# The last w_down rows as two column halves, three pieces loaded in parts by partitions, and 4 MB of w_o as one load

## Chip, cores and metric

One core of one Trainium2 chip. The time is the device time of one execution in microseconds (us), the median of several; the times of the kernel before lie within 0.1% of each other in one set of runs.

## The reference, cut to what matters

A decode step of one token: adaLN modulation, attention of 32 query heads over a cache of 4 x 65536 positions, then a gated feed-forward. The end of it is what the change touches:

```python
def _B_ref(x, w_gate, w_up, w_down):          # x: 1 x 1024, F = 3584
    return _gelu(x @ w_gate) * (x @ w_up) @ w_down
...
h = _layernorm(x, axis=-1) * (1 + cb) + sb
x = x + gb * _B_ref(h, B_w_gate, B_w_up, B_w_down)
```

Every weight and every cache row is used once, so the kernel is a stream of 185.6 MB from HBM into SBUF with the arithmetic beside it.

## The kernel before

All loads are planned in one list and issued in that order from SP. Each goes into a slot of a ring, is a single transfer over all 128 partitions, and adds 16 to a semaphore (the trace has 16 landing records for each of the last pieces):

```python
def issue_ready():
    while issued[0] < len(loads):
        j = loads[issued[0]]
        if any(q.freed is None for q in j.prev):
            return
        SP.wait(*(q.freed for q in j.prev))
        sp.dma_start(j.view, j.src).then_inc(j.tok[0], 16)
        issued[0] += 1
```

w_down comes last. The list, with the cuts of the last two blocks of 512 rows:

```python
j_o += [plan_o(16, 0), plan_o(24, 1)]                    # w_o: two of 2 MB
... # w_gate: two of 3.67 MB; w_up: two of 3.67 MB
wd_v = B_w_down.rearrange("(b p e) n -> p b e n", p=P, e=UE)   # b: 7 blocks, p: 128 partitions, e: 4 rows
... # two loads of two blocks (2 MB each), then
while b < NBF:
    for e, ne in ((0, UE),) if b < NROW else ((0, 2), (2, 2)) if b == NROW else ((0, 2), (2, 1), (3, 1)):
        ...  # 1 MB | 512 KB, 512 KB | 512 KB, 256 KB, 256 KB
```

The first five blocks are used as the moving operand (row matmuls, 512 columns); the last two as weights, so that the output falls into columns of PSUM that need no transpose:

```python
for kk in range(nk):
    for j in range(nblk):                                # nblk = 8
        ins = pe.matmul(
            bank[:, j:j + 1], view[:, kk, j:D:nblk], rhs[:, k0 + kk:k0 + kk + 1],
            start=first, stop=True, skip_group_check=True)
```

`view[:, kk, j:D:nblk]` is 128 weight columns, 8 elements (16 bytes) apart.

## Time and profile before

| | kernel before |
|---|---|
| time | 437.44 us (437.43 to 437.52, 3 runs) |
| span of the profiled run, granted clock | 436.2 us, 0.830 |
| HBM read | 185.60 MB at 426 GB/s over the span |
| landing of the 1 MB piece | 428.38 us |
| landing of the three 512 KB pieces | 429.62, 430.89, 432.13 us |
| landing of the two 256 KB pieces | 432.76, 433.40 us |
| end of the last matmul | 434.3 us |

A landing is the time at which the last of a load's 16 shares has come, read from its semaphore in the trace. TensorE in the last 8 us, as the timeline of the kernel before has it (start and length in us, engine, line, operation, tiles, shapes, count, and in brackets the idle time before it with what ended it):

```profile
428.42 1.06 PE L409 MATMUL kt_ps<-slots,p_row 128*32 128x512 bf16 x8 [1.38 <-DMA slots<-in_B_w_down_dram]
429.67 1.13 PE L386 MATMUL b<-p_row,slots 128*128 128x1 bf16 x16 [0.19 <-DMA slots<-in_B_w_down_dram]
430.92 0.29 PE L868 MATMUL b<-kt_sb,sel 128*32 128x8 f32 x8
431.14 3.14 PE L386 MATMUL b<-p_row,slots 128*128 128x1 bf16 x48
```

After 428.42 the brackets almost disappear: 48 column matmuls run without one. The windows of the kernel before (length, busy us of each engine with its count, granted clock, mean share of the DMA engines that are busy, GB/s) show the loads at their full rate almost to the end:

```profile
427.00:428.00 1.00, 0.04 (x4) 0.00 (x0) 0.00 (x0) 0.00 (x0) 0.00 (x0) 0.84 0.99 410
429.00:430.00 1.00, 0.81 (x13) 0.34 (x6) 0.45 (x1) 0.00 (x0) 0.00 (x0) 0.50 1.00 410
430.00:431.00 1.00, 0.88 (x20) 0.80 (x20) 0.86 (x2) 0.00 (x0) 0.00 (x0) 0.50 1.02 406
```

### The profile page before, as it was taken

To read this page: it belongs to the slowest core of one execution; us is meant where nothing else is said; L and a number is where in the kernel's file an instruction comes from. 1 tells how busy PE (TensorE), PEld (TensorE's weight loads), DVE (VectorE), ACT (ScalarE), POOL (GpSimd) and SP (SyncE) were. 2 spreads that over 40 slices of the span, in tenths; PEclk is the share of its full clock that TensorE was granted. 3 is DMA by queue.
4 is the path that set the end of the run, shared out by engine and by line. 5 is a ranking of instruction groups with operands and counts; after the bars stand their busy time and mean duration, and the time that the engine had idled before them with its cause. 6 is when DMAs were issued, how large, how long until landed. Compare 5 with 4: busy or idle time off the path is not lost.

```text
span 436.2 us, 8423 instructions
## 1 busy us (share of the span) xinstructions
PE 302.8 (69%) x3858; PEld 200.5 (46%) x3858; DVE 206.7 (47%) x303; ACT 111.2 (26%) x164; POOL 16.8 (4%) x23
## 2 busy tenths in 40 slices
PE   0435559959696878949787794969689596565366
PEld 0112236736464656636465563646456373232024
DVE  6601015637373755736474763738377465321001
ACT  1000001533332423333341353333235334000000
POOL 9500000000000000000000000000000000000000
PEclk9995569999796988988896897969689889578856
DMA  8999999999999999999999999999999999999996
GB/s 355 433 421 434 433 431 431 431 432 433 433 433 439 430 433 433 436 433 433 439 433 433 433 430 436 433 436 436 433 433 433 433 418 436 437 433 429 420 425 265
DMA packets 8192, 185.77 MB, mean 426 GB/s; under 512 B 1010, under 2 KB 1010, under 8 KB 1652
## 3 DMA queue, kind: packets, MB, share of 16 engines
q1 hardware_dynamic: 8176, 185.60, 99.0%
q8 instruction: 8, 0.13, 0.1%
q14 instruction: 4, 0.03, 0.0%
q10 hardware_dynamic: 4, 0.00, 0.0%
HBM read 185.60 MB, written 0.00 MB: 426 GB/s over the span
## 4 chain that ended last, share of the span: by engine, by line
DMA 56%; PE 31%; DVE 11%; issue 1%; ACT 1%; POOL 0%; POOLq 0%
DMA slots<-in_A_k_cache_dram 45%; PE kt_ps L575 16%; DMA slots<-in_B_w_down_dram 7%; PE b L645 4%; DMA slots<-in_A_v_cache_dram 4%; PE sc_ps L597 4%; PE kt_ps L409 3%; DVE selt L359 3%; DVE kt_sb L683 2%; DVE s_pad L717 1%; DVE o_red L706 1%; PE sc_ps L626 1%; PE b L613 1%; PE b L386 1%; DVE o_acc L694 1%
## 5 line engine op out<-in xcount | busy, mean ns | idle before, releaser
L575 PE MATMUL kt_ps<-ident,slots 128*128 128x128 bf16 x2048 | 156.7, 238 | 48.8 <-DMA slots<-in_A_k_cache_dram 48.0
L683 DVE COPY kt_sb<-kt_ps 128x2048 bf16<-128x2048 bf16 x96 | 117.6, 1225 | 111.5 <-PE kt_ps L575 109.9
L575 PEld LDWEIGHTS kt_ps<-ident,slots 128*128 128x128 bf16 x2048 | 136.1, 108 | 74.3 <-issue 41.9
L683 ACT ACTIVATE kt_sb<-kt_ps 128x2048 bf16<-128x2048 bf16 x32 | 60.1, 1877 | 27.7 <-PE kt_ps L575 27.7
L732 ACT ACTIVATE p_sb<-sc_ps 128x512 bf16<-128x512 bf16 x32 | 19.1, 597 | 182.4 <-PE sc_ps L626 182.4
L597 PE MATMUL sc_ps<-kt_sb,q_buf 128*32 128x512 bf16 x528 | 50.8, 420 | 0.0
L645 PE MATMUL b<-slots,p_sb 128*32 128x512 bf16 x560 | 40.1, 411 | 5.3 <-DMA slots<-in_A_v_cache_dram 4.6
L409 PE MATMUL kt_ps<-slots,h_pad 128*32 128x512 bf16 x176 | 19.1, 571 | 22.0 <-DMA slots<-in_B_w_up_dram 9.7
L694 DVE SCALAR_TENSOR_TENSOR o_acc<-o_acc,s_pad,b 128x512 f32<-128x512 f32 x28 | 20.9, 747 | 12.2 <-PE b L645 11.9
L613 PE MATMUL b<-m_sp,selt 128*128 128x16 f32 x66 | 13.0, 272 | 18.2 <-DVE m_sp L722 16.5
L645 PEld LDWEIGHTS b<-slots,p_sb 128*32 128x32 bf16 x560 | 15.5, 104 | 20.1 <-issue 5.1
L717 DVE TENSOR_REDUCE s_pad<-sc_ps 128x1 f32<-128x512 f32 x32 | 21.8, 682 | 0.0
L738 ACT ACTIVATE p_row<-sc_ps,s_pad 128x512 bf16<-128x512 f32 x32 | 21.7, 677 | 0.0
L409 PEld LDWEIGHTS kt_ps<-slots,h_pad 128*32 128x32 bf16 x176 | 6.3, 130 | 32.7 <-issue 11.9
L613 PEld LDWEIGHTS b<-m_sp,selt 128*128 128x128 f32 x66 | 9.8, 188 | 23.7 <-DVE m_sp L722 21.4
L597 PEld LDWEIGHTS sc_ps<-kt_sb,q_buf 128*32 128x32 bf16 x528 | 10.9, 95 | 12.3 <-issue 4.5
L409 PE MATMUL kt_ps<-slots,s_pad 128*32 128x512 bf16 x96 | 10.9, 516 | 7.5 <-DMA slots<-in_w_mod_dram 7.5
L452 POOL TENSOR_TENSOR rs<-va,halfneg 128x1 f32<-128x1 f32 x2 | 1.1, 555 | 375.7 <-DVE va L449 375.7
L793 DVE COPY kt_sb<-kt_ps 128x512 f32<-128x512 f32 x3 | 2.1, 692 | 27.7 <-PE kt_ps L409 27.7
L626 PEld LDWEIGHTS sc_ps<-ident,p_row 128*128 128x128 bf16 x136 | 7.8, 98 | 15.1 <-issue 14.4
L626 PE MATMUL sc_ps<-ident,p_row 128*128 128x128 bf16 x136 | 13.7, 224 | 0.2 <-ACT p_row L738 0.2
L727 DVE TENSOR_REDUCE s_pad<-b 128x1 f32<-128x16 f32 x32 | 5.6, 175 | 14.6 <-PE b L613 14.6
(98 smaller groups left out, 148.1 us busy)
## 6 DMA issues: line engine op xcount, KB each, us to landing
slots<-in_A_k_cache_dram SPq DMA_DIRECT2D x16, 4096.0 KB, 23.5
slots<-in_A_v_cache_dram SPq DMA_DIRECT2D x16, 4096.0 KB, 23.6
slots<-in_w_mod_dram SPq DMA_DIRECT2D x4, 3072.0 KB, 20.4
slots<-in_A_wq_dram SPq DMA_DIRECT2D x2, 4096.0 KB, 35.8
slots<-in_A_wo_dram SPq DMA_DIRECT2D x4, 2048.0 KB, 25.3
slots<-in_B_w_gate_dram SPq DMA_DIRECT2D x2, 3584.0 KB, 30.2
slots<-in_B_w_up_dram SPq DMA_DIRECT2D x2, 3584.0 KB, 29.5
slots<-in_B_w_down_dram SPq DMA_DIRECT2D x2, 2048.0 KB, 35.1
```

Of the source, the lines that this page charges most:

```text
L359: dve.tensor_scalar(selt[:, :].rearrange("p (r h) -> p r h", h=REP), selw[:, HQ - REP:HQ].unsqueeze(1).to_broadcast([P, NR, REP]), -scale, ...
L409: ins = pe.matmul(out, pad[:, k, :], view[:, kk, c0:c0 + ROW], start=k <= last_k[0], stop=k >= last_k[1], skip_group_check=True,)
L575: ins = pe.transpose(kt_ps[:, half * 2048 + t * P:half * 2048 + (t + 1) * P], j_k[i - i % KU].view[:, i % KU * CH + b * TB + t, :], ident[ ...
L597: ins = pe.matmul(sc(j)[QD * g:QD * (g + 1), :], q_buf[:, j % SITES, QD * b:QD * (b + 1)], kt_sb[:, j % 2, n:n + w, :].rearrange("p n d -> ...
L613: ins = pe.matmul(b6[:, 0:NR], selt[:, :], m_sp[:, j % 2, :], start=True, stop=True)
L626: ins = pe.transpose(sc_bf[:, o:o + P], p_row[:, j % 2, c * P:(c + 1) * P], ident[:, :])
L645: ins = pe.matmul(b7[QD * c:QD * (c + 1), :].rearrange("p (b d) -> p b d", b=NB), p_sb[:, s, c * P + QD * g:c * P + QD * (g + 1)], v[:, NQ ...
L683: ev[i % SITES][b].done(act.activation(dst, src, ACT.Copy) if E_ is AC else dve.tensor_copy(dst, src))
L694: v = oc[j % SITES].done(dve.scalar_tensor_tensor(o_acc[:, :], o_acc[:, :], al[:, j:j + 1], b7[:, :], ALU.mult, ALU.add))
L717: v = DVE.done(dve.tensor_reduce(m_new, sc(j), AX.X, ALU.max))
L732: pc[jt % SITES].done(act.activation(p_sb[:, jt % SITES, :], sc_bf[:, o:o + ROW], ACT.Copy))
L738: v_x[j] = ex[s].done(act.activation(p_row[:, j % 2, :], sc(j), ACT.Exp, bias=mneg[:, j:j + 1], scale=scale, accum_out=zr[:, j:j + 1],))
```

## The change

Its intent: the 16 DMA engines run dry at different times, up to 1.8 us apart (the shares of the last load land from 431.60 to 433.40), and a cut of 112 rows plus a few is meant to give the late ones less; the last 256 KB come as two column halves, so that less work is left after the last landing; and w_o's last two loads of 2 MB become one of 4 MB. The core of the diff:

```diff
-            sp.dma_start(j.view, j.src).then_inc(j.tok[0], 16)
+            p = 0
+            for n in j.cut:
+                sp.dma_start(j.view[p:p + n], j.src[p:p + n]).then_inc(j.tok[0], 16)
+                p += n
...
-        j_o += [plan_o(16, 0), plan_o(24, 1)]
+        j_o.append(plan_o(16, 0, 16))
...
                     jb = plan_load(
-                        wd_v[:, b, e:e + ne, :], flat(ne, D), jb.slot, beside=jb, off=(UE + e) * D, sem=9 - e)
+                        wd_v[:, b, e:e + ne, :], flat(ne, D), jb.slot, beside=jb, off=(UE + e) * D, sem=9 - e,
+                        cut=(112, 12, 4) if e == 0 else (112, 14, 2))
+                elif b + 1 == NBF and e == 0:
+                    jb = plan_load(wd_v[:, b, e:e + ne, :], flat(ne, D), next(tail_d), cut=(112, 10, 6))
+                elif b + 1 == NBF and e + 1 == UE:
+                    halves = [plan_load(
+                        wd_v[:, b, e:e + 1, h * ROW:(h + 1) * ROW], flat(1, ROW), next(tail_d)) for h in range(2)]
+                    break
...
-        v = col_matvec(acc_dn, late[1:], o_pad[:, :, 0], KD, False)
+        col_matvec(acc_dn, late[1:], o_pad[:, :, 0], KD, False)
+        for h, jb in enumerate(halves):
+            PE.wait(jb.tok)
+            for j in range(KD):
+                ins = pe.matmul(
+                    acc_dn[h * P // 2:(h + 1) * P // 2, j:j + 1], jb.view[:, 0, j:ROW:KD], o_pad[:, FD - 1:FD, 0],
+                    start=False, stop=True, skip_group_check=True)
```

More of the change, by code (lines that the diff above doesn't have):

```diff
@@ L198, in bass_adaLN_cond__gqa_block_cached__geglu_ffn__decode_kernel, with plan_load @@
     loads = []
-    def plan_load(src, view_fn, slot, site=None, nslot=1, beside=None, off=0, sem=None):
+    def plan_load(src, view_fn, slot, site=None, nslot=1, beside=None, off=0, sem=None, cut=(P,)):
         if site is not None:
@@ L206, in plan_load @@
             sem = slot if sem is None else sem
-            nfill[sem] += 1
+            nfill[sem] += len(cut)
             tok = (fill[sem], 16 * nfill[sem])
@@ L210, in plan_load @@
         job.src = src
+        job.cut = cut
         job.freed = None
@@ L264, in emit_all, with plan_o @@
         tail = iter([2, 4, 6, 8])
-        tail_d = iter([0, 1, 2, 3, 4, 5])
-        def plan_o(k, slot):
-            return (plan_load(wo_v[:, k:k + 8, :], flat(8, D), slot), k, 8)
+        tail_d = iter([0, 1, 2, 3, 4, 5, 6])
+        def plan_o(k, slot, n=8):
+            return (plan_load(wo_v[:, k:k + n, :], flat(n, D), slot, nslot=n // 8), k, n)
         def vslot(j):
@@ L870, in emit_all @@
                 start=False, stop=True, skip_group_check=True)
-        v = col_matvec(acc_dn, late[1:], o_pad[:, :, 0], KD, False)
+        col_matvec(acc_dn, late[1:], o_pad[:, :, 0], KD, False)
[5 more added lines that the diff above has]
+                    start=False, stop=True, skip_group_check=True)
+            v = PE.done(ins)
+            release(jb, v)
         DVE.wait(v)
```

## The prediction

> **What bounds the kernel now.** I read the page first, for the whole span.
>
> ```profile
> PEclk9995569999796988988896897969689889578856
> DMA  8999999999999999999999999999999999999996
> HBM read 185.60 MB, written 0.00 MB: 426 GB/s over the span
> DMA slots<-in_A_k_cache_dram 45%; PE kt_ps L575 16%; DMA slots<-in_B_w_down_dram 7%; PE b L645 4%; DMA slots<-in_A_v_cache_dram 4%; PE sc_ps L597 4%; PE kt_ps L409 3%; DVE selt L359 3%; DVE kt_sb L683 2%; DVE s_pad L717 1%; DVE o_red L706 1%; PE sc_ps L626 1%; PE b L613 1%; PE b L386 1%; DVE o_acc L694 1%
> ```
>
> The DMA engines are full in 38 of 40 slices: the kernel streams 185.6 MB, and neither kernel reads less. Only the two ends can move. So I read the chain of waits of the last 10 us (start, length, what):
>
> ```profile
> 397.44 30.93 DMA slots<-in_B_w_down_dram
> 428.38 0.04 issue
> 428.42 1.10 PE kt_ps L409 x8
> 429.52 0.03 issue
> 429.55 1.33 DVE kt_sb L860 x2
> 430.87 0.04 issue
> 430.92 0.29 PE b L868 x8
> 431.21 3.09 PE b L386 x48
> 434.30 0.02 issue
> 434.32 0.18 DVE kt_sb L873
> 434.50 0.02 issue
> 434.52 0.17 DVE kt_sb L875
> ```
>
> The last load on this chain is the 1 MB piece that lands at 428.38. Five pieces (three of 512 KB, two of 256 KB) land after it and are not on the chain. From 428.42 everything is TensorE and VectorE work: eight row matmuls, two transposes, four fp32 matmuls, 48 column matmuls in one run, then VectorE and the store.
>
> Is a load nearly on it? The trace has, for every load, the landing of each of its 16 shares. The last shares come at 429.62, 430.89, 432.13, 432.76 and 433.40. Instruction by instruction, TensorE reaches the matmuls that need them at 429.66, 431.14, 432.08, 433.13 and 433.61. It waits 0.09 us (start 432.175) for the third 512 KB piece; it comes 0.37 us after the first 256 KB piece and 0.2 us after the last one. The stretches of these column matmuls say the same (length, busy us and count, clock, DMA share, GB/s):
>
> ```profile
> core 0: us, PE busy (x) PEld busy (x), PEclk, DMA share, GB/s
> 431.13:432.15 1.02, 1.01 (x16) 1.01 (x16) 0.50 0.79 301
> 432.15:433.10 0.95, 0.95 (x18) 0.95 (x17) 0.50 0.41 155
> 433.10:433.60 0.50, 0.50 (x11) 0.50 (x11) 0.50 0.00 0
> 433.60:434.30 0.70, 0.68 (x12) 0.60 (x10) 0.50 0.00 0
> ```
>
> TensorE is full from 431.13 to the end while DMA falls away from 0.79 to nothing. The end is a TensorE chain, with 0.2 us of slack at the last load.
>
> DMA runs out unevenly. Following the packets engine by engine, six engines finish between 431.30 and 431.59, two at 431.97 and 432.10, eight between 432.78 and 433.09. The mean is 432.26, so a perfect levelling would end the loads 0.84 us sooner. The offsets are old: each appears at an instruction fetch (8 packets of 16 KB on queue 8, some of 8 KB on queue 14), which holds one engine back by 0.87 to 0.95 us, or 0.3, and stays. This is what the cut of 112 + a few rows addresses.
>
> [...]
> [...] The trace shows small pieces at nearly the full rate: packets of 32, 16, 8, 4 and 2 KB start every 1209, 607, 306, 155 and 80 ns, about 5 ns plus 37.5 ns per KB.
> [...] the column matmuls read their weights as 4 chunks of 32 columns, and follow each other every 60 ns; 128-column fp32 weights (L470) are read in one run of 128 and come every 109 to 114 ns, some 0.86 ns a column.
>
> **The change part by part.**
> 1. w_o as one load: per engine, 16 packets of 607 and two completions of 6 ns become 8 of 1209 and one: 9724 - 9678 = 46 ns of stream saved. The three landings around it (377.36, 382.21) are ahead of the matmuls that use them (383.53), so that wait costs nothing. Slots 0 and 1 are freed together, so one w_down load is issued about 0.9 us later; it has 33 us of queue ahead of it. All w_down pieces should land up to 0.05 us sooner.
> 2. The cuts (112,12,4), (112,14,2), (112,10,6): same bytes; [...] A row is 155 ns, [...] the last landing gains between 0 and 0.31 us (433.09 - 432.78), and the third 512 KB piece about as much. Worth on the chain: only TensorE's 0.09 us wait.
> 3. Six more issues in SP here and one in the halves, less one for w_o. SP already stands in its issues (7.4, 6.6 and 2.4 us for the last three)[...]; the last issue ends at 415.96. [...]
> 4. The halves: 16 packets of 1 KB at about 42.5 ns (estimate from the line above) and two completions, 692 ns, for 8 x 80 + 6 = 646: +0.05 us for the last landing.
> 5. Matmuls: eight of 128 weight columns become 16 of 64. Without the four chunks, 64 x 0.86 = 55 ns each, or the present 60: 16 x 55 to 60 = 0.88 to 0.96 us in place of 8 x 60 = 0.48. All 16 are on the chain if the halves have landed: +0.40 to +0.48. The first half is reached at about 433.55 and the second at 434.0, against landings near 433.1 to 433.4.
>
> Sum: -0.05 (stream) - 0.05 (of the 0.09 wait) + 0.44 (weights) = +0.3 us, and a bit less if the smaller loads overlap better than I think: I take +0.2. The prediction is 437.65 us.
>
> **The rivals.**
> A: the tail is bound by DMA, as the change supposes. Then levelling brings 0.3 us and the half-size last piece 0.2 more: 437.0. Against it: no wait of TensorE at the last two pieces.
> B: the cuts slow the loads. [...] If each cut piece took 0.3 us more, the third would land 0.9 us late, TensorE would wait, and the time would be 438.3.
> C: 64 columns load in half the time of 128 (30 ns): 16 x 30 = 8 x 60, and only the 0.1 us of parts 1 and 2 remains: 437.3. The 27 ns between 128-column loads at L780 (32 rows, unit stride) says that TensorE can issue so fast; the strided 60 ns speaks against.
> [...]
>
> **Range and chances.** C and A together reach 437.0 to 437.3, B 438.3. The three times before lie within 0.09 us, so noise is small. 80% range: 437.1 to 438.2. Two per cent is 8.7 us, more than the whole tail after the 1 MB piece (7.8 us from 428.4 to 436.2): a larger change needs an accident.
>
> **What would show it.** Right: TensorE busy without a gap from the first 512 KB pieces to the end, 64-column matmuls every 55 to 60 ns, both halves landed before TensorE asks; landing spread of the last piece near 1.0 to 1.4 us in place of 1.8. Wrong: a wait on a half or on the third 512 KB piece (A or B by its sign), a spacing near 30 ns (C), or pieces of 512 KB further apart than 1.24 us (B). The prediction fails altogether if an issue of SP runs past 430.

The sum came to -0.05 - 0.05 + 0.44 = +0.34 us, told as +0.3 and taken as +0.2: 437.65. Cut too are the estimate of where SP's issues end, and a fourth rival, D, on the order of the engines, which came to the same time.

## The result, and the profile after

442.44 us (442.03 to 442.95, 5 runs) against 437.46 (437.43 to 437.52, 5 runs) of the kernel before: ratio 1.0114, 95% interval 1.0099 to 1.0129. 5.0 us were added where the prediction had 0.2, and the range ended at 438.2.

The chain of waits of the kernel after, its last 28 us (start, length, what):

```profile
413.91 22.21 DMA slots<-in_B_w_down_dram
436.12 0.05 issue
436.17 1.61 PE b L397 x24
437.78 1.57 PE b L886 x16
439.35 0.02 issue
```

Before, the chain left the loads at 428.38. Now it leaves them at 436.12, with the landing of the third 512 KB piece: 3.99 us later than that piece landed before (432.13). From that landing to the end of the matmuls it takes 3.2 us (436.17 to 439.35), against 2.1 before (432.175 to 434.28): 1.07 more. The two make the 5.0 us. The timeline of TensorE shows where it now stands:

```profile
429.70 1.05 PE L420 MATMUL kt_ps<-slots,p_row 128*32 128x512 bf16 x8 [1.75 <-DMA slots<-in_B_w_down_dram]
432.09 1.13 PE L397 MATMUL b<-p_row,slots 128*128 128x1 bf16 x16 [1.33 <-DMA slots<-in_B_w_down_dram]
434.15 1.14 PE L397 MATMUL b<-p_row,slots 128*128 128x1 bf16 x16 [0.71 <-DMA slots<-in_B_w_down_dram]
436.17 1.61 PE L397 MATMUL b<-p_row,slots 128*128 128x1 bf16 x24 [0.88 <-DMA slots<-in_B_w_down_dram]
437.71 1.62 PE L886 MATMUL b<-p_row,slots 128*64 128x1 bf16 x16
```

There is a wait in front of the 1 MB piece and of each of the three 512 KB pieces; the last 256 KB piece and the halves had landed when TensorE came to them. Why the loads are late is in the windows of the kernel after:

```profile
424.00:426.00 2.00, 0.74 (x8) 0.00 (x0) 0.00 (x0) 0.00 (x0) 0.00 (x0) 0.50 1.02 430
427.00:428.00 1.00, 0.95 (x12) 0.04 (x4) 0.00 (x0) 0.00 (x0) 0.00 (x0) 0.50 0.98 242
430.00:431.00 1.00, 0.76 (x8) 0.00 (x0) 0.18 (x1) 0.00 (x0) 0.00 (x0) 0.50 1.08 246
432.00:433.00 1.00, 0.91 (x15) 0.92 (x16) 0.14 (x1) 0.00 (x0) 0.00 (x0) 0.50 1.04 262
```

The two last columns say it: the DMA engines are as busy as before (0.98 to 1.08), and they move 242 to 262 GB/s where they moved 406 to 410. By their busy share the engines do not wait for work; each packet takes longer. In the trace before, all 384 packets of 4 KB took 159 ns; after, their median is 254 ns and the longest 434. Here the share of busy time did not tell the two rates apart: 1.00 stood beside 410 GB/s before, 0.98 beside 242 after.

The landings, us:

| | before | after |
|---|---|---|
| 1 MB piece (not cut itself) | 428.38 | 429.66 |
| 512 KB pieces | 429.62, 430.89, 432.13 | 432.04, 434.11, 436.12 |
| 256 KB; then 256 KB (before) or two halves (after) | 432.76; 433.40 | 436.51; 436.83, 437.14 |

### The profile page after: what moved, and what is told of

Same layout as the page of the kernel before. It is cut to its first block, busy times and chain, and to the rows that moved or that the text cites. A ratio compares the mean times of both kernels' runs of the same rounds, so it can differ in the third digit from the quotient of the medians. Undisturbed runs are those within 1.5% of the kernel's fastest.

```text
span 441.2 us, 8445 instructions
## 1 busy us (share of the span) xinstructions
PE 307.9 (70%) x3866; PEld 202.3 (46%) x3866; DVE 206.6 (47%) x303; ACT 111.2 (25%) x164; POOL 16.8 (4%) x23
## 4 chain that ended last, share of the span: by engine, by line
DMA 53%; PE 31%; DVE 10%; SPq 3%; issue 1%; ACT 1%; POOL 0%; POOLq 0%
DMA slots<-in_A_k_cache_dram 44%; PE kt_ps L586 16%; DMA slots<-in_B_w_down_dram 5%; PE b L656 5%; PE sc_ps L608 4%; DMA slots<-in_A_v_cache_dram 4%; PE kt_ps L420 3%; SPq L234 3%; DVE selt L370 3%; DVE kt_sb L694 2%; DVE s_pad L728 1%; DVE o_red L717 1%; PE sc_ps L637 1%; PE b L624 1%; DVE o_acc L705 1%
## 5 line engine op out<-in xcount | busy, mean ns | idle before, releaser
L608 PEld LDWEIGHTS sc_ps<-kt_sb,q_buf 128*32 128x32 bf16 x528 | 11.0, 95 | 12.5 <-issue 4.9
L420 PE MATMUL kt_ps<-slots,p_row 128*32 128x512 bf16 x104 | 10.7, 574 | 3.9 <-DMA slots<-in_B_w_down_dram 3.1
```

Source lines behind the costliest of these rows:

```text
L420: ins = pe.matmul(out, pad[:, k, :], view[:, kk, c0:c0 + ROW], start=k <= last_k[0], stop=k >= last_k[1], skip_group_check=True,)
L608: ins = pe.matmul(sc(j)[QD * g:QD * (g + 1), :], q_buf[:, j % SITES, QD * b:QD * (b + 1)], kt_sb[:, j % 2, n:n + w, :].rearrange("p n d -> ...
```

## The experiments

Thirteen kernels. Where a result is wrong it is said. Experiments 1 to 4 share one chip and the runs of the kernel before (437.57 us, 437.47 to 437.68, 7 runs), 10 to 12 another (437.56 us, 437.31 to 437.76, 9 runs).

**1. w_o alone as one load.**

```diff
-        j_o += [plan_o(16, 0), plan_o(24, 1)]
+        j_o.append(plan_o(16, 0, 16))
```

> Only the single 4 MB load of w_o. All theories agree that it carries nothing of the +5.0 us: 437.4 to 437.5. In the profile after the change the loads behind it land within 0.06 us of those before, so my 0.05 us gain should not show either. A time above 437.8 would make the late freeing of slots 0 and 1 a suspect.

Measured: 437.5 us (437.4 to 437.65, 4 runs), ratio 0.9998 (0.9982 to 1.0015). This part does nothing that can be seen.

**2. The halves alone.** The change's `halves` and their 16 matmuls; every other load whole.

```diff
+                        cut=(P,))                        # in place of (112, 12, 4) and (112, 14, 2)
...
+                    jb = plan_load(wd_v[:, b, e:e + ne, :], flat(ne, D), next(tail_d), cut=(P,))
+                elif b + 1 == NBF and e + 1 == UE:
+                    halves = [plan_load(
+                        wd_v[:, b, e:e + 1, h * ROW:(h + 1) * ROW], flat(1, ROW), next(tail_d)) for h in range(2)]
```

> Only the column halves of the last row. Theory W (64-column strided weight loads cost 120 ns each, as the profile after the change shows inside one half, against 60 ns for 128 columns): about +1.0 us, 438.3 to 438.6, with the loads landing as before and TensorE running without a gap to the end. My prediction's step 5 (55 to 60 ns): 437.9. Rival: the two 128 KB loads are what slows the loads, +4 us or more.

Measured: 438.6 us (438.45 to 438.62, 4 runs), ratio 1.0023 (1.0006 to 1.004). The loads land as before (third 512 KB piece 432.19, last half 433.51, all 4 KB packets 159 ns; in the profile of experiment 1, which has no halves, the last two are 432.25 and 433.51). The timeline of this kernel:

```profile
431.22 2.62 PE L397 MATMUL b<-p_row,slots 128*128 128x1 bf16 x40
433.78 1.62 PE L886 MATMUL b<-p_row,slots 128*64 128x1 bf16 x16
```

No wait before either line: both halves had landed. 40 matmuls with 128 weight columns take 2.62 us (about 65 ns each), 16 with 64 columns 1.62 us (101 ns each over the group; within one half they follow each other every 120 ns). So the halves cost 1.03 us, all of it on TensorE.

**3. The cuts alone.** w_o and the last piece as before.

```diff
+                        cut=(112, 12, 4) if e == 0 else (112, 14, 2))
...
+                    jb = plan_load(wd_v[:, b, e:e + ne, :], flat(ne, D), next(tail_d), cut=(112, 10, 6))
```

> Only the three pieces cut by partitions. Theory P ([...] everything in flight slows to about 250 GB/s): about +4.0 us, 441.2 to 441.6, the third 512 KB piece landing near 436.1 in place of 432.13, and packets of 4 KB taking about 250 ns in place of 159. If the cuts are innocent and it is the sum of small loads: under 439.

Measured: 441.48 us (441.19 to 441.65, 4 runs), ratio 1.0089 (1.0072 to 1.0106); the third piece lands at 436.15, 4 KB packets have a median of 255 ns. Cuts 3.9, halves 1.0, w_o 0: the sum is 4.9 of the 5.0 us.

**4. The same pieces cut into 112 and 16.** The small uneven loads are gone: each piece is one load of 112 rows and one of 16.

```diff
+                        cut=(112, 16))
...
+                    jb = plan_load(wd_v[:, b, e:e + ne, :], flat(ne, D), next(tail_d), cut=(112, 16))
```

> The same three pieces cut 112 + 16[...]. Theory P1 (the 112 rows themselves are the cause): as slow as the cuts alone, 440.8 to 441.8. Theory P2 (the small loads[...] are the cause[...]): near 437.5, with 4 KB packets at 159 ns.

Measured: 440.84 us (440.55 to 441.34, 4 runs), ratio 1.0076 (1.0059 to 1.0092); the third piece lands at 435.63, the median packet of 4 KB takes 255 ns. So 3.3 of the 3.9 us come of loading 112 rows and 16 rows at all. The uneven small loads, which were the aim of the cut, are no faster than the even one: some 0.6 us slower in the medians, though the two ranges overlap (441.19 to 441.65 against 440.55 to 441.34), and there are three loads in place of two.

The theory formed here, a supposition that no run had shown yet: the rows of SBUF that a load goes to set its rate. The expectations of 5 to 8 call it P (in 5 and 6 the rate falls with the number of rows); those of 9 and 13 call it M, and there it counts which rows they are: rows 32 to 95 at the whole rate, rows 0 to 63 at half. Its rivals: HBM or the number of loads is the limit; or every load of fewer than 128 rows is slow (N). The next experiments take loads seven times larger, where the tail's other waits play no part.

**5. A w_gate load as 64 + 64 rows, a w_up load as four of 32.** (each 3.67 MB; the other load of each matrix stays whole)

```diff
+        big = iter([(64, 64), (128,), (32, 32, 32, 32), (128,)])
-        j_g = [(plan_load(wg_v[:, k:k + 4, :], flat(4, F), next(tail), nslot=2), k, 4) for k in range(0, KD, 4)]
+        j_g = [(plan_load(wg_v[:, k:k + 4, :], flat(4, F), next(tail), nslot=2, cut=next(big)), k, 4)
+               for k in range(0, KD, 4)]
... # j_u likewise
```

> The kernel before, but the first w_gate load (3.67 MB) is issued as 64 + 64 partitions and the first w_up load as four times 32; all loads [...] keep their 28 KB packets. Theory P [...]: [...] w_gate's first load takes about 17 us in place of 8.5, and [...] w_up's first load takes up to 34 us; in all 455 to 472 us. Rival S (only small packets, or rows that are not a multiple of four, are slow): both loads stay at 8.5 us and the time at 437.5.

Measured: 461.71 us against 437.63. The second load of 64 rows (1.83 MB) lands 9.3 us after the first: 197 GB/s. The loads of 32 rows (0.92 MB each), as far as no whole load was beside them, land 4.1 and 4.5 us apart: some 215 GB/s. One window of this kernel:

```profile
390.00:400.00 10.00, 1.54 (x10) 1.27 (x10) 2.58 (x13) 0.60 (x1) 0.55 (x1) 0.81 0.99 208
```

The expectation of up to 34 us for the load in four parts of 32 rows (a quarter of the rate) was wrong: 32 and 64 rows run alike, at half of the whole load's 430.

**6. 112 + 16 and 96 + 32 rows at the same places.**

```diff
+        big = iter([(112, 16), (128,), (96, 32), (128,)])
```

> The same with the first w_gate load as 112 + 16 partitions and the first w_up load as 96 + 32, 28 KB packets. Theory P: 112 rows run at about 0.6 of the full rate as the 4 KB pieces did (250 of 430 GB/s), and the 16 rows slower still, so that w_gate's first load takes 12 to 16 us in place of 8.5 and w_up's 12 to 18; total 444 to 455 us. Rival S: what was slow was the 4 KB packet size with cuts; here 437.5.

Measured: 460.65 us against 437.63, above the range that was expected. The 112 rows take 14.1 us, the 16 rows 4.85; the 96 rows 12.5, the 32 rows 5.2. For 112, 96, 32 and 16 of 128 rows the share of the 8.5 us that a whole load takes (experiment 13) would be 7.4, 6.4, 2.1 and 1.1 us: the parts take 1.9 to 4.6 times that, the small ones the most. The longest packet took 3.73 us, 3.5 times the 1.06 us that a packet of this size (28,672 bytes) takes in the kernel before (median of 512).

**7 and 8. Destination or source?** The two 2 MB loads of w_down as four loads of 512 KB each. In 7 they go to 64 partitions at a time; in 8 (wrong result: rows land in other partitions than the matmuls take them for) contiguous pieces of the same HBM region go to all 128.

```diff
+    jb.parts = [(jb.view[64 * a:64 * a + 64, bb, :, :], wd_v[64 * a:64 * a + 64, b + bb, :, :])   # 7
+                for bb in range(2) for a in range(2)]
...
+    jb.parts = [(jb.view[:, bb, 2 * a:2 * a + 2, :].rearrange("p e n -> p (e n)"),                # 8
+                 B_w_down[(2 * (b + bb) + a) * 256:(2 * (b + bb) + a + 1) * 256, :]
+                 .rearrange("(p h) n -> p (h n)", h=2)) for bb in range(2) for a in range(2)]
```

> The two 2 MB w_down loads as eight loads of 512 KB, each one unbroken run of memory into 64 partitions (8 KB packets). Theory P: these 4 MB take about 19 us in place of 9.8, so 445 to 448 us. If the place in HBM decides, the next run is as slow.

> The same eight 512 KB runs of memory, each put into all 128 partitions as 4 KB packets (the result is wrong on purpose). Theory P (the destination partitions decide): full rate, 437.5 to 438. Rival H (which HBM rows are read together, or merely the number of loads, decides): as slow as the run before it, 445 or more.

Measured: 446.43 us (7) and 437.58 us (8), against 437.63. The windows, first of 7, then of 8:

```profile
420.00:424.00 4.00, 3.07 (x24) 1.46 (x17) 0.72 (x2) 0.59 (x1) 0.00 (x0) 0.67 1.01 246
```

```profile
420.00:424.00 4.00, 2.26 (x24) 1.40 (x24) 0.75 (x3) 0.36 (x1) 0.00 (x0) 0.99 1.03 423
```

The same bytes of HBM, in as many loads of the same size, move at 246 GB/s to 64 partitions and at 423 to 128. The rivals "HBM" and "number of loads" fall. (The packets differ too, 8 KB in 7 and 4 KB in 8; but in the kernel before both sizes ran at their full rate, 309 and 159 ns, and in 7 the 8 KB packets from 415 us on take 534 ns in the median.) It also shows that loads of 512 KB cost nothing that can be seen by being small.

**9. Middle rows between outer ones.** By M a load of rows 32 to 95 should run at the full rate, though it has no more rows than that of rows 0 to 63.

```diff
+        big = iter([(32, 64, 32), (128,), (48, 64, 16), (128,)])
```

> The kernel before with the first w_gate load as 32 + 64 + 32 partitions (0-31, 32-95, 96-127) and the first w_up load as 48 + 64 + 16. Theory M [...]: rows 32-95 [...] load in about 4.2 us, half the time of rows 0-63 (9.3 us measured), while rows 48-111 [...] take about 8.5; the 48 rows take some 9 us, the 32 rows 4.2 each and the 16 rows 4.2. w_gate's load 12.7 us, w_up's about 22, total 455. Rival N (any load under 128 partitions[...]): both 64-row parts take 8.5 to 9.3 us.

Measured: 464.96 us against 437.56, ten more than expected. From 389 to 390 us, where rows 32 to 95 were nearly alone in flight, packets took 1062 to 1068 ns; but most of their time they shared with the loads of 32 rows beside them (from 391 to 394 us packets took 2.1 to 3.5 us). The parts of the w_up load are mixed in the same way. The total decides nothing, and experiment 13 repeats the question without parts that lie side by side in time.

**10. Finer whole pieces.** Not part of the change: if small loads cost nothing (8), six pieces of 256 KB at the end, behind one of 512 KB, should let TensorE begin earlier. The edit also puts the four fp32 matmuls behind the second piece (not shown in the cut).

```diff
-  ((0, 2), (2, 2)) if b == NROW else ((0, 2), (2, 1), (3, 1)):
+  ((0, 2), (2, 1), (3, 1)) if b == NROW else ((0, 1), (1, 1), (2, 1), (3, 1)):
```

> An attempt at a version faster than both: no partition cuts, no halves; the last pieces are whole-width loads of one or two rows (512 KB, then six of 256 KB), and the four fp32 matmuls stand after the second piece, so that TensorE works in the 0.3 us in which it waited for the transposes. Worked out from the landings before: 437.3, a gain of 0.1 to 0.2 us; three more loads cost 0.05 us each of stream. If TensorE's chain is not what binds, the time stays at 437.5 or rises by 0.1.

Measured: 437.48 us (437.43 to 437.54, 5 runs), ratio 0.9998 (0.9984 to 1.0012): no gain. The last landing moves from 433.40 to 433.58, and TensorE is busy to the end as before (40 column matmuls from 431.49 to 434.29 without a wait). The added piece has a semaphore of its own.

**11. The halves with neighbouring columns.** Wrong result: each matmul takes 64 columns side by side in place of every eighth.

```diff
-   jb.view[:, 0, j:ROW:KD]
+   jb.view[:, 0, j * P // 2:(j + 1) * P // 2]
```

> The halves alone, but each takes 64 neighbouring weight columns in place of every eighth one (the result is wrong on purpose). Theory W1 (the stride of 16 bytes doubles the cost of a column: 1.9 ns strided, 0.9 not): 55 to 60 ns per 64-column load inside one half in place of 120, and about 438.0. Theory W2 (only the loss of the four-chunk read counts): 120 ns and 438.6 as before.

Measured: 437.76 us (437.75 to 437.96, 4 runs), ratio 1.0006 (0.9991 to 1.0022), so 0.2 us over the kernel before where the halves of experiment 2 cost 1.03. The timeline, to be set beside that of experiment 2:

```profile
433.73 0.83 PE L886 MATMUL b<-p_row,slots 128*64 128x1 bf16 x16
```

0.83 us in place of 1.62; within one half the matmuls follow each other every 53 ns in place of 120. The stride of 16 bytes makes some 0.8 of the 1.03 us.

**12. Neighbouring columns in all column matmuls, loads as before.** Wrong result.

```diff
-   view[:, kk, j:D:nblk]
+   view[:, kk, j * P:(j + 1) * P]
```

> The kernel before, but all 64 column matmuls take 128 neighbouring weight columns (wrong on purpose). Theory W1: about 30 ns each in place of 60, TensorE no longer binds the tail but the last landing does: 433.4 + 8 x 0.03 + 0.2, so 437.0 to 437.1. This measures what the tail could gain at most while the loads land as they do. Theory W2: 60 ns and 437.5.

Measured: 437.11 us (436.98 to 437.13, 4 runs), ratio 0.9989 (0.9974 to 1.0004). The timeline:

```profile
431.17 0.58 PE L393 MATMUL b<-p_row,slots 128*128 128x1 bf16 x16
432.23 0.98 PE L393 MATMUL b<-p_row,slots 128*128 128x1 bf16 x24 [0.47 <-DMA slots<-in_B_w_down_dram]
433.46 0.37 PE L393 MATMUL b<-p_row,slots 128*128 128x1 bf16 x8 [0.26 <-DMA slots<-in_B_w_down_dram]
```

128 neighbouring columns take 0.58 us for 16 matmuls (1.13 with stride), one every 27 ns (60 with stride): the stride doubles this path too. So there are two factors, each of about two. At either stride a matmul with 64 columns takes about twice the time of one with 128 (53 against 27 ns, 120 against 60), and at either width the stride takes about twice the time of neighbouring columns. Now TensorE waits for the last landing. About 0.45 us (437.56 to 437.11; the ranges do not overlap, though the interval of the ratio just holds 1) is the most that TensorE can win here while the loads land as they do; a correct kernel of this kind needs another layout of the output vector throughout, and was not made.

**13. Middle rows alone, lower rows alone.** Wrong result: of one w_gate load only rows 32 to 95 come, of one w_up load only rows 0 to 63, each between whole loads.

```diff
+        big = iter([slice(32, 96), None, slice(0, 64), None])
...
+            sp.dma_start(j.view[r], j.src[r]).then_inc(j.tok[0], 16)
```

> Wrong result on purpose: of the first w_gate load only partition rows 32 to 95 are loaded, of the first w_up load only rows 0 to 63; both are 1.83 MB in 28,672-byte packets and lie between whole loads of 128 rows. Theory M [...]: rows 32 to 95 land about 4.3 us after the load before them, at the whole load's rate, with packets of about 1062 ns; rows 0 to 63 take about 8.5 us with packets of about 2.1 us; the total is about 433.3 us, 4.2 under the kernel before. Rival N (any load of 64 partitions runs at half rate, whichever they are): both take 8.5 to 9.3 us, and the total is 437.5 to 438.

Measured: rows 32 to 95 land 4.30 us after the load before them; every packet of 28,672 bytes that started from 380 to 388 us took 1062 ns. Rows 0 to 63 land 8.83 us after the load before them, with packets of 2.06 to 2.33 us. Windows of this kernel, the first two in the middle rows and the whole load behind them, the last two in rows 0 to 63:

```profile
384.00:386.00 2.00, 2.00 (x24) 0.85 (x20) 0.00 (x0) 0.00 (x0) 0.00 (x0) 0.50 1.03 444
386.00:387.00 1.00, 1.00 (x13) 0.34 (x8) 0.00 (x0) 0.00 (x0) 0.00 (x0) 0.50 1.00 430
398.00:400.00 2.00, 2.00 (x30) 0.85 (x23) 0.00 (x0) 0.00 (x0) 0.00 (x0) 0.80 0.98 201
400.00:402.00 2.00, 1.21 (x13) 0.86 (x8) 0.69 (x1) 0.59 (x1) 0.00 (x0) 1.00 0.93 201
```

As many rows, as many bytes, DMA engines nearly as busy (1.00 and 1.03 against 0.98 and 0.93): 430 to 444 against 201 GB/s. The rate follows which rows are loaded, and the rival "any load under 128 partitions" falls. Why these rows and not those is not shown by any run. The total, 435.35 us against 437.54, is 2.2 us lower, not the 4.2 that M had expected. The missing 2 us are in the whole load ahead of rows 0 to 63: it lands 10.4 us after the middle rows, where whole loads land 8.5 apart. The lower rate begins at about 393 us (387 GB/s from 392 to 394, 229 from 394 to 396), before the whole load lands (at about 397: 8.83 us before rows 0 to 63, which TensorE starts on at 405.87). 83 packets of these loads take over 1.7 us, although the half load has only 64: so at least 19 of a whole load's are stretched too. A half load slows its neighbour as well, as the 1 MB piece was slowed by 1.28 us in the kernel after.

## Why the prediction was wrong

Step by step, in its own order.

1. *w_o as one load, -0.05 us.* Right in what matters: nothing to be seen in the time (experiment 1). The gain of 0.05 was not seen either: its last landing in the kernel after is 382.26, against 382.21.

2. *The cuts: "same bytes", a row of 155 ns, worth at most the 0.09 us wait.* This step failed, and 4 of the 5 us are in it. It took the 155 ns of a row as given, whatever the load's shape. With 112 and fewer rows the packets of 4 KB took 254 ns in the median. The third 512 KB piece came 3.99 us late, and TensorE, which had 0.09 us of waiting to lose, gained waits of 1.33, 0.71 and 0.88 us. Experiment 4 puts 3.3 us on loads of 112 and 16 rows as such; 5, 7, 8 and 13 put it on the rows of the destination: 197 to 246 GB/s into the rows 0 to 63 or 64 to 127, 423 to 444 into all 128 or into rows 32 to 95. The levelling that the step forecast did not come: the shares of the last load land from 434.78 to 437.14, 2.36 us apart, where the prediction looked for 1.0 to 1.4 in place of 1.8.

3. *SP's issues end near 421.* Right, though the author's estimate is cut above with the packet count behind it: the last one ended at 420.87, and the prediction's own alarm (an issue after 430) did not sound.

4. *The halves' stream, +0.05 us.* It was not on the chain, as said. Its size can't be told: experiment 2 has the last landing at 433.51 for 433.40, but so has experiment 1 without halves.

5. *The halves' matmuls: 16 of 55 to 60 ns, +0.44 us.* The kind of cost was right (TensorE chain, no wait for a half, the 64 columns read in one run where the 128 are read as four chunks of 32, in the trace after) and the size was off: 120 ns each, and 1.03 us for the part. The mis-sized term is the 0.86 ns a column, which came from 128-column weights read in one run with unit stride; the halves are read at a stride of 16 bytes, and experiment 11 shows that the stride is the difference (53 ns without it, for the 55 that were predicted).

**The rivals.** B ("the cuts slow the loads") was the right one. It was sized with a number that was made up: 0.3 us per piece, 0.9 in all, and 438.3 us. No trace that was there before the result could size it; experiment 4 measures 3.3 us. A (DMA-bound, levelling helps) fell: its premise, loads on the path, came true only because the loads became slower. C fell with the 120 ns, and would have fallen without the stride too: 53 ns (11), not 30. D stays open: the packet records name no engine, and in the kernel after, where packets are stretched, following them from one to the next is not certain, so whether the late engines got fewer rows is not shown.

That the levelling does not pay is shown (experiment 3 is no faster than 4, and the last load's shares land further apart than before). Why it does not pay is not shown by any run.

**The range.** 437.1 to 438.2 was built from rivals that agreed that a load's shape matters by tenths of a microsecond. The sentence that a larger change "needs an accident" had no measurement behind it: no load of the kernel before has fewer than 128 partitions, except for two of one row, so its trace could not speak on the main item of the change. That was a reason for a wide range.

## What to carry to other kernels

Before cutting a load by partitions, measure the rate of each part in a run: 64 rows from 0 ran at 201 GB/s, 64 rows from 32 at 430, 112 rows took nearly twice the time of their share (14.1 us for 7.4). Cut a stream by columns or by rows per partition instead; pieces of 512 and 256 KB over all 128 partitions cost nothing here (423 GB/s in experiment 8, 437.48 us in experiment 10). And a DMA share of 1.0 in the windows was not a full stream here (0.98 beside 242 GB/s): read the GB/s beside it, and when they part, the packet times.
